# Two of 24 sums of spectra products moved from VectorE to accumulating transfers that GpSimd issues

## The chip, the cores and the metric

The kernel runs on one core of a Trainium2 chip. The metric is device time in microseconds (us) of one execution. Of the kernel before, three runs gave 275.06, 275.24 and 275.45 us; the median is 275.24 us. A further execution was profiled. It took 275.08 us, of which the profile's span, from the first to the last instruction of the program, is 273.3 us; the other 1.8 us lie around it.

A core has five engines that run side by side and tell each other of finished work through semaphores: TensorE (PE: matmuls, with weight loads listed apart as PEld), VectorE (DVE), ScalarE (ACT), GpSimd (POOL) and SyncE (SP, which only issues transfers). Each works through its own instructions in their order. Sixteen DMA engines carry out the transfers.

## The reference

The input `x` is `A_u`, 2048 positions of 640 channels in bf16. Two branches read it and are mixed by a gate for each position:

```python
g = _sigmoid((x * gate_w).sum(-1, keepdims=True))
a = _A_ref(x, A_re, A_im, B_re, B_im, C_re, C_im, log_dt, Dskip)
b = (_gelu(x @ w_gate) * (x @ w_up)) @ w_down        # F = 1728
return g * a + (1 - g) * b
```

`_A_ref` builds for each channel a filter `K` of 2048 lags (128 complex exponentials, summed) and convolves `x` with it along the positions, by the product of their spectra, then adds `u * Dskip`:

```python
K = jnp.einsum("dn,dnl,dn->dl", Cc, P, dB).real      # P = exp(dt * A * l)
Yf = Uf * Kf                                         # spectra of u and K, complex
y = irfft2(Yf)[..., :L].astype(bfloat16) + u * Dskip
```

## The kernel before, in words

**Spectra in blocks.** The kernel cuts the 2048 positions into four blocks of 512 and the filter in the same way. Matmuls with constant cosine and sine matrices make the spectra `Uf[i]` of the blocks and `Kf[j]` of the filter's parts (steps `U...` and `K...`, lines 729 and 742; ScalarE takes them out of PSUM). Output block `c` is the sum over pairs of blocks `i` and filter parts `j = c - i` of complex products. This is done for the channels in two halves `h` of 320. A spectrum tile is 128 partitions of 2 x 4 x 320 values.

**The products.** The function `spectra(c)` does this on VectorE. Names are made of `h`, `c`, `i` and a part: `m0110` is a product for half 0, block 1, input block 1, part 0. Part 0 goes to a tile `P` (two buffers, by `c % 2`), part 1 to `X`. The first pair of a block writes its product straight into `P` or `X` (line 784, 128x2560). Each further pair writes its product into a tile `t` or `t1` (line 787) and is then added: step `s...`, line 788. There are 24 such sums in all. At the end `y...0` and `y...1` (lines 790 and 791, 128x1280) combine `P` and `X` crosswise, and `P` holds the finished spectrum.

**The inverse.** Matmuls with `P` as the moving data bring the block back to positions (`I...`, line 802, 8 matmuls a step). They must end before `P`'s buffer is written for the block after the next.

**The other branch.** Its matmuls run first (line 391); up-products are kept in HBM (`Ud`), come back through a ring of three buffers on the SP queue (`rl...`, line 717) and are multiplied into `H` on VectorE (`hm...`, line 718, 128x1024). `H` is the weight of the down matmuls (`D...`, line 816), which add into the same PSUM as the mixing of the first branch (`Z...`, lines 823 and 824); ScalarE scales and SP stores.

**Order.** All of it is written out by hand: the string `ORDER` is a list of step names, and the steps are issued in its order. Engines keep the order of their own steps; which one waits for which follows from the tiles that they touch. GpSimd has little to do: some memsets and, early on, eight gathers (line 375).

Of the kernel before, what the change touches and what calls it, by code (L numbers as in the profile page):

```python
# [11 lines left out]
ALU = mybir.AluOpType  # L12
# [54 lines left out]
eK010/A ge5.0 ek1.5/D ct1.2/1 ct1.1/2 gl3 lu01 rl10.0 lw13 ct1.6/3 ek1.4/D gl4 ek1.2/D hm4.0 ge1.0 ek1.1/A lwz0 gl5 ct1.0/0  # L67
ek1.0/A hm5.0 gl6 ct1.3/1 ek1.6/A ek1.3/D ge11.0 K002/2 U011/3 eK002/D K012 eK012/A ge12.0 U010/0 eU010/A rl12.0 U013/1
eU013/A gl7 ks.1 m0000 kd.1 g8.1/2 rl2.0 m0001 hm10.0 leu3 eU011/A dg8 rl1.0 gf/1 U012/3 eU012/A ge3.0 y000 g9.1/2 gf1 ge7.0
m0101 y001 g11.1/3 lkb1 lu02 K022/1 U022/0 dg9 gl8 lim1 U021/2 m0100 lkb0 hm12.0 dg11 rl7.0 hm1.0 m0111 leu0 eU022/A K033/3  # L70
eU021/A U023/0 er0 lim0 hm2.0 K020/2 rl3.0 eK033/A eK022/A eU023/A lu03 eK020/A I001/3 s0101 eI001/A rl6.0 U020/1 m0110
K023/0 hm7.0 s0100 rl0.0 g10.1/2 lu10 hm3.0 rl8.0 eU020/A U032/1 ge9.0 y011 eK023/A eU032/A m0221 y010 U030/3 rg0.1 leu1 er1
eU030/A hm6.0 I000/0 U031/1 hm0.0 K021/3 dg10 rl9.0 m0210 U103/2 hm8.0 rl11.0 m0211 eI000/A rg13.1 eU031/A rl13.0 rg7.1 m0220
rg6.1 eU103/A D000/0 K030/1 eK021/A K031/2 hm9.0 eK030/A D000a rg5.1 eK031/A hm11.0 U100/1 ge13.0 eU100/A D001/2 lwe0 er2
K032/3 eK032/A rl11.1 pm0/A hm13.0 pm1/A D001a U101/1 eU101/A I010/3 D000b ge13.1 D001b U033/1 D000c s0220 eI010/A D001c
# [5 lines left out]
eU111/A K101/3 eU122/A hm1.1 lwz1 U120/2 K120/0 eK123/A lwe1 eU120/A rl0.1 rl3.1 s0311 s0310 hm2.1 eK101/A lu13 hm0.1 eK120/A  # L81
hm3.1 U123/1 D021/2 m0320 eU123/A m0321 K111 D020/1 eK111/A U133/3 s0320 K130/0 D021a D020a eK130/A pm3/A pm2/A eU133/A lwd1
s0321 m0330 m0331 s0330 s0331 st010 m1000 U131/0 Z021 D031/3 y030 o021/A eU131/A st021 U121/0 Z020 o020/A y031 D031a I031/1
m1100 eU121/A st020 D030/2 I030/0 eI030/A D030a m1001 m1101 y100 y101 eI031/A Z031 Z030 o030/A o031/A I101/1 m1110 m1111
s1100 s1101 I100/0 eI101/A U132/3 m1210 y111 y110 m1221 m1211 m1220 s1221 s1220 eU132/A D100/1 eI100/A m1201 K132/2 D101/3
U130/0 D101a D100a eU130/A Z101 m1200 Z100 eK132/A s1201 st030 o101/A o100/A st100 s1200 I111/2 m1321 y121 D111/3 I110/0
D111a D110/1 eI111/A D130/2 y120 m1310 m1311 m1320 s1321 Z111 D110a o111/A eI110/A K133/3 eK133/A Z110 st031 o110/A s1320
I121/0 I120/3 m1331 eI121/A m1330 D120/1 D130a s1331 s1330 K131/0 eK131/A m1301 m1300 s1301 eI120/A s1300 st110 st101 st111
# [56 lines left out]
def kernel(  # L145
# [25 lines left out]
    V, A, P, S, G = nc.vector, nc.scalar, nc.tensor, nc.sync, nc.gpsimd  # L171
# [87 lines left out]
    def step(name, fn, job=None, opening=False):  # L259
        assert name not in steps, name  # L260
        steps[name] = fn
        if opening:
            opens[name] = job
# [7 lines left out]
    for i in range(6):  # L271
        step(f"lp{i}", lambda i=i: (A if i == 0 else S).dma_start(out=at["prm"][:, i],
                                                                 in_=PRM[i].rearrange("(p j) n -> p (j n)", p=128)))
# [53 lines left out]
    tt, ts, stt = V.tensor_tensor, V.tensor_scalar, V.scalar_tensor_tensor  # L327
# [333 lines left out]
    for th in range(2):  # L661
        step(f"er{2 + th}", lambda th=th: tt(out=H[th][64:78, 13].rearrange("q (x p) -> q x p", x=2)[:, :, 508:512],
                                             in0=edge_r[64:78, 2 * th:2 * th + 2], in1=edge[:, 2 * th:2 * th + 2], op=ALU.mult))
# [30 lines left out]
    for h in range(2):  # L694
# [3 lines left out]
                                       op=ALU.mult))  # L698
# [49 lines left out]
    for h in range(2):  # L748
# [22 lines left out]
        def spectra(c, h=h, Uf=Uf, Kf=Kf):  # L771
            Pt, X, tb = at["P"][:, c % 2], at["X"], (at["t"], at["t1"])
            fl = (lambda v: v.rearrange("p r m d -> p r (m d)"))
            seq = PAIRS[h][c]
            flip0 = (c - seq[0]) % 2
            for i in seq:
                j = c - i
                for part in range(2):
                    dst, t = (Pt, X)[part], tb[part]
                    row = part ^ (j % 2)  # L780
                    ux = fl(Uf[i])[:, row:row + 1].to_broadcast([128, 2, 4 * W2])
                    kx = fl(Kf[j])
                    if i == seq[0]:
                        step(f"m{h}{c}{i}{part}", lambda dst=dst, ux=ux, kx=kx: tt(out=fl(dst), in0=ux, in1=kx, op=ALU.mult))
                    else:
                        op = ALU.subtract if part and j % 2 != flip0 else ALU.add
                        step(f"m{h}{c}{i}{part}", lambda t=t, ux=ux, kx=kx: tt(out=fl(t), in0=ux, in1=kx, op=ALU.mult))
                        step(f"s{h}{c}{i}{part}", lambda t=t, dst=dst, op=op: tt(out=fl(dst), in0=fl(dst), in1=fl(t), op=op))  # L788
            ops = (ALU.add, ALU.subtract) if flip0 else (ALU.subtract, ALU.add)
            step(f"y{h}{c}0", lambda: tt(out=fl(Pt)[:, 0], in0=fl(Pt)[:, 0], in1=fl(X)[:, 1], op=ops[0]))  # L790
            step(f"y{h}{c}1", lambda: tt(out=fl(Pt)[:, 1], in0=fl(Pt)[:, 1], in1=fl(X)[:, 0], op=ops[1]))
# [69 lines left out]
        for c in range(4):  # L861
            spectra(c)
            inverse(c)
# [38 lines left out]
```

## Time and profile before

| what | value |
|---|---|
| median of three runs | 275.24 us (275.06 to 275.45) |
| profiled execution | 275.08 us, span 273.3 us |
| TensorE busy in the span | 261.3 us |
| VectorE busy | 255.6 us |
| ScalarE busy | 219.4 us |
| GpSimd busy | 36.7 us |
| moved by DMA | 49.05 MB, mean 179 GB/s |
| one sum of a product (line 788), 24 of them | 1.48 us each |

The page of a profile gives shares over the whole span; the kernel has stages with different limits, so a stage is read from the table of busy time by stretch, and the order within it from the timeline. A row of the timeline has the start and the duration in us, the engine, the line, the operation, what it writes and reads, how many instructions are merged in it, and in brackets the engine's idle time ahead of it with what ended it. An instruction's duration holds its tail in the pipeline; the next one starts a little before it ends, so what an instruction costs its engine is the distance to the next start.

### The profile page before, as it was taken

How to read it: one execution, taken by the hardware profiler on the slowest of the kernel's cores; microseconds unless marked ns; L12 is line 12 of the kernel's file. 1: busy time of each engine (PE TensorE's matmuls, PEld its weight loads, DVE VectorE, ACT ScalarE, POOL GpSimd, SP SyncE). 2: the span in 40 equal slices, each digit the busy share in tenths (PEclk: the TensorE clock that was granted, in tenths of full speed). 3: DMA queues.
4: the chain of work that ended last, by engine and by line, in shares of the span. 5: the costliest groups of instructions: out<-in, count | busy, mean ns of one | idle time of the engine just before them, and what ended most of it. 6: DMA issues, size and time to landing. Idle time of an engine off the chain costs nothing.

```text
span 273.3 us, 4927 instructions
## 1 busy us (share of the span) xinstructions
PE 261.3 (96%) x1874; PEld 159.8 (58%) x1889; DVE 255.6 (94%) x330; ACT 219.4 (80%) x300; POOL 36.7 (13%) x23
## 2 busy tenths in 40 slices
PE   4899999999999999999998999999999999999995
PEld 3743444444674444555594557777777777777773
DVE  0899999999989999999999999999999999999971
ACT  3899999999999999999999999999985444305223
POOL 2300301999531000000010000000000000000000
PEclk9999999999999999999999999999999999999999
DMA  7968859864785888887995896978980100101011
GB/s 196 261 184 227 250 140 242 276 208 105 195 272 139 233 265 245 246 287 210 276 288 121 280 252 195 289 202 267 262 246 23 50 0 26 46 2 50 24 50 48
DMA packets 64141, 49.05 MB, mean 179 GB/s; under 512 B 23499, under 2 KB 52982, under 8 KB 64118
## 3 DMA queue, kind: packets, MB, share of 16 engines
q1 hardware_dynamic: 63158, 47.00, 61.0%
q0 software_dynamic: 384, 1.31, 1.8%
q10 hardware_dynamic: 576, 0.43, 0.5%
q8 instruction: 15, 0.25, 0.4%
q14 instruction: 8, 0.07, 0.1%
HBM read 30.44 MB, written 15.67 MB: 169 GB/s over the span
## 4 chain that ended last, share of the span: by engine, by line
PE 71%; ACT 18%; DVE 5%; issue 3%; DMA 2%; SPq 0%; DVEq 0%; ACTq 0%
PE ps L391 24%; PE ps L816 22%; PE ps L802 6%; PE ps L729 6%; PE ps L742 4%; ACT work L396 3%; DVE work L398 2%; ACT work L480 2%; PE ps L537 2%; PE ps L538 2%; ACT work L472 2%; ACT H L709 2%; PE ps L823 2%; ACT work L484 2%; PE ps L824 1%
## 5 line engine op out<-in xcount | busy, mean ns | idle before, releaser
L391 PE MATMUL ps<-xT,Wr 128*128 128x512 bf16 x525 | 118.9, 379 | 3.7 <-DVE work L347 0.7
L391 PEld LDWEIGHTS <-Wr 128*128 128x128 bf16 x540 | 52.6, 98 | 65.7 <-issue 5.0
L396 ACT CAST work<-ps 128x640 bf16<-128x640 f32 (+1 forms) x59 | 47.5, 838 | 11.5 <-PE ps L802 7.4
L375 POOL DMA_INDIRECT early<-in_A_u_dram,back x8 | 31.4, 3929 | 40.7 <-DVE early L382 32.3
L816 PE MATMUL ps<-xT,H 128*128 128x320 bf16 x224 | 32.9, 299 | 0.0
L402 ACT ACTIVATE Wr<-ps,gs 128x320 bf16<-128x320 f32 x30 | 14.0, 527 | 23.0 <-PE ps L824 14.7
L816 PE MATMUL ps<-xT,work 128*128 128x320 bf16 x224 | 32.4, 299 | 0.0
L816 PEld LDWEIGHTS <-H 128*128 128x128 bf16 x224 | 21.9, 98 | 8.5
L816 PEld LDWEIGHTS <-work 128*128 128x128 bf16 x224 | 21.9, 98 | 8.5
L504 ACT ACTIVATE tail<-work 128x1920 bf16<-128x1920 int16 x14 | 25.3, 1821 | 0.4
L525 DVE TENSOR_TENSOR work<-tail,work 128x1920 bf16<-128x1920 bf16 (+1 forms) x22 | 23.4, 1087 | 0.0
L507 ACT ACTIVATE tail<-work 128x1920 bf16<-128x1920 int16 (+1 forms) x12 | 19.5, 1631 | 1.5 <-DVE work L487 1.0
L802 PE MATMUL ps<-work,tail 128*128 128x320 bf16 x128 | 19.5, 299 | 0.0
L492 DVE SCALAR_TENSOR_TENSOR work<-early,tail 128x320 int32<-128x320 f32 x42 | 18.0, 481 | 0.0
L788 DVE TENSOR_TENSOR work<-work,early 128x2560 bf16<-128x2560 bf16 x12 | 17.8, 1481 | 0.0
L788 DVE TENSOR_TENSOR work<-work 128x2560 bf16<-128x2560 bf16 x12 | 17.8, 1480 | 0.0
L729 PEld LDWEIGHTS <-early 128*128 128x128 bf16 x128 | 12.5, 98 | 7.6 <-issue 2.3
L516 DVE TENSOR_TENSOR work<-tail,work 128x1920 bf16<-128x1920 bf16 x14 | 16.1, 1150 | 0.2
L487 DVE TENSOR_SCALAR work<-work 128x960 int32<-128x960 int16 (+1 forms) x26 | 16.1, 624 | 0.1
L398 DVE CAST work<-ps 128x1024 bf16<-128x1024 f32 x13 | 15.7, 1212 | 0.0
L742 PE MATMUL ps<-KTt,early 128*128 128x320 bf16 x80 | 15.5, 299 | 0.0
L802 PEld LDWEIGHTS <-tail 128*128 128x128 bf16 x128 | 12.5, 98 | 4.9
(128 smaller groups left out, 423.1 us busy)
## 6 DMA issues: line engine op xcount, KB each, us to landing
Ud<-work SPq DMA_DIRECT2D x26, 256.0 KB, 2.4
work<-Ud SPq DMA_DIRECT2D x26, 256.0 KB, 3.3
Wr<-in_B_w_gate_dram SPq DMA_DIRECT2D x10, 320.0 KB, 3.7
Wr<-in_B_w_up_dram SPq DMA_DIRECT2D x10, 320.0 KB, 3.9
PMd<-early SPq DMA_DIRECT2D x4, 640.0 KB, 4.9
Gd<-work SPq DMA_DIRECT2D x9, 256.0 KB, 4.7
work<-Gd SPq DMA_DIRECT2D x9, 256.0 KB, 5.0
out_dram<-Wr SPq DMA_DIRECT2D x14, 160.0 KB, 1.9
```

The lines of the kernel that those rows point to most:

```text
L375: G.indirect_dma_start(out=at["ur"][:, e, :], out_offset=None, in_=u2[:, :], in_offset=bass.IndirectOffsetOnAxis(ap=back[:, 2 * c + e:2 * ...
L391: P.matmul(t[:, x, :], lhsT=Wr[:, slot, kt, cols:cols + 128], rhs=xT[:, th, kt, 512 * x:512 * x + 512], start=(kt == 0), stop=(kt == 4))
L396: A.copy(out=out, in_=in_)
L398: V.tensor_copy(out=out, in_=in_)
L504: act(out=T, in_=low16(t)[:, :, :, ::2], func=ACT.Sin, scale=SIN_SCALE)
L507: act(out=T[:, :, 0:n], in_=low16(t[:, :, 0:n])[:, :, :, ::2], func=ACT.Sin, scale=SIN_SCALE)
L525: tt(out=B2[:, :, :, cols].rearrange("p r g x -> p g r x"), in0=Tv if hf == 0 else Tv[:, :, ::-1], in1=e, op=ALU.mult)
L729: P.matmul(t[:, r, 0:W2], lhsT=FM[:, m, e, r], rhs=pm[:, r, e], start=(e == 0), stop=(e == 1))
L742: P.matmul(t[:, r, 0:W2], lhsT=mat[:, r], rhs=KTt[:, q, d], start=(x == 0 and j != 1), stop=(x == len(seq) - 1), skip_group_check=(j == 1))
L788: step(f"s{h}{c}{i}{part}", lambda t=t, dst=dst, op=op: tt(out=fl(dst), in0=fl(dst), in1=fl(t), op=op))
L802: P.matmul(t[:, r, 0:W2], lhsT=IM[:, e, m, r], rhs=Y[:, r, m], start=(m == 0), stop=(m == 3))
L816: P.matmul(t[:, x, 0:W2], lhsT=H[c // 2][:, ft, tk:tk + 128], rhs=at[f"Wd{h}"][:, ft], start=(ft == 0), stop=False)
```

## The change

Two things are changed. For block `c = 1`, in both halves, the sum of part 0 (`s0100` and `s1100`) is no longer an addition on VectorE. GpSimd issues a transfer from `t` to `P` in which the DMA engines add the source to what stands at the destination. And the list of steps is put in another order around both: the products `m0110` and `m1110`, which write `P` first, come earlier, and the transfer stands right behind them.

```diff
-m0101 y001 ... m0100 lkb0 hm12.0 dg11 rl7.0 hm1.0 m0111 leu0 eU022/A K033/3
-eU021/A U023/0 er0 lim0 hm2.0 ... I001/3 s0101 eI001/A rl6.0 U020/1 m0110
-K023/0 hm7.0 s0100 rl0.0 g10.1/2 lu10 hm3.0 rl8.0 ... y011
+m0101 y001 ... m0100 lkb0 hm12.0 dg11 rl7.0 hm1.0 m0111 m0110 s0100 leu0
+eU022/A K033/3 eU021/A U023/0 er0 lim0 hm2.0 ... I001/3 s0101 eI001/A rl6.0
+U020/1 K023/0 hm7.0 rl0.0 g10.1/2 lu10 hm3.0 rl8.0 ... y011
...
-m1100 eU121/A ... m1001 m1101 y100 y101 ... m1110 m1111
-s1100 s1101 I100/0 eI101/A U132/3 m1210 y111 y110
+m1100 eU121/A ... m1001 m1101 m1110 s1100 y100 y101 ...
+m1111 s1101 I100/0 eI101/A U132/3 m1210 y111 y110
...
-                        step(f"s{h}{c}{i}{part}", lambda t=t, dst=dst, op=op: tt(out=fl(dst), in0=fl(dst), in1=fl(t), op=op))
+                        if part == 0 and c == 1:
+                            step(f"s{h}{c}{i}{part}", lambda t=t, dst=dst: G.dma_start(out=fl(dst), in_=fl(t), accum_op=ALU.add,
+                                                                                       max_dma_last_dim=2560))
+                        else:
+                            step(f"s{h}{c}{i}{part}", lambda t=t, dst=dst, op=op: tt(out=fl(dst), in0=fl(dst), in1=fl(t), op=op))
```

Four lines are added, so lines from 788 on carry a number that is higher by 4 in the changed kernel: 788 becomes 792 (and 789 the transfer), 790 and 791 become 794 and 795, 802 becomes 806, 816 becomes 820.

On VectorE around the first sum the order was, with the semaphores that each row waits for (L784: `m0111`, `m0110`; L788: `s0101`, `s0100`; L791: `y011`; L718: H products):

```order
L784 TENSOR_TENSOR work<-work,early 128x2560 [waits DVE_49,Activation_49]
L718 TENSOR_TENSOR H_78<-H_78,work 128x1024 [waits DMAHW1_49,Activation_49]
L788 TENSOR_TENSOR work<-work,early 128x2560 [waits DVE_49]
L784 TENSOR_TENSOR work<-work,early 128x2560
L718 TENSOR_TENSOR H_78<-H_78,work 128x1024 [waits DMAHW0_49,Activation_49]
L788 TENSOR_TENSOR work<-work 128x2560 [waits DVE_49]
L718 TENSOR_TENSOR H_78<-H_78,work 128x1024 [waits DMAHW4_49]
L791 TENSOR_TENSOR work<-work 128x1280 [waits DVE_49]
```

and with the change:

```order
L784 TENSOR_TENSOR work<-work,early 128x2560 [waits DVE_49,Activation_49]
L784 TENSOR_TENSOR work<-work,early 128x2560
L718 TENSOR_TENSOR H_78<-H_78,work 128x1024 [waits DMAHW1_49,Activation_49]
L792 TENSOR_TENSOR work<-work,early 128x2560 [waits DVE_49]
L718 TENSOR_TENSOR H_78<-H_78,work 128x1024 [waits DMAHW0_49,Activation_49]
L718 TENSOR_TENSOR H_78<-H_78,work 128x1024 [waits DMAHW4_49]
L795 TENSOR_TENSOR work<-work 128x1280 [waits DMASW0_49,DVE_49]
```

One L788 is gone, the second L784 stands directly behind the first, and the combine L795 now waits for a semaphore of the GpSimd queue's transfers (`DMASW0`).

Around the second sum VectorE had this order (L784: `m1110`, `m1111`, `m1210`; L790 and L791 are first `y100`, `y101`, and at the end `y111`, `y110`):

```order
L787 TENSOR_TENSOR early<-tail,work 128x2560
L790 TENSOR_TENSOR work<-work 128x1280 [waits DVE_49]
L791 TENSOR_TENSOR work<-work 128x1280
L784 TENSOR_TENSOR work<-early,tail 128x2560 [waits PE_49]
L784 TENSOR_TENSOR work<-early,tail 128x2560 [waits DVE_49]
L788 TENSOR_TENSOR work<-work 128x2560 [waits DVE_49]
L788 TENSOR_TENSOR work<-work,early 128x2560 [waits DVE_49]
L784 TENSOR_TENSOR work<-early,work 128x2560 [waits PE_49]
L791 TENSOR_TENSOR work<-work 128x1280 [waits DVE_49]
```

and has this one with the change:

```order
L787 TENSOR_TENSOR early<-tail,work 128x2560
L784 TENSOR_TENSOR work<-early,tail 128x2560 [waits PE_49]
L794 TENSOR_TENSOR work<-work 128x1280 [waits DVE_49]
L795 TENSOR_TENSOR work<-work 128x1280
L784 TENSOR_TENSOR work<-early,tail 128x2560 [waits DVE_49]
L792 TENSOR_TENSOR work<-work,early 128x2560 [waits DVE_49]
L784 TENSOR_TENSOR work<-early,work 128x2560 [waits PE_49]
L795 TENSOR_TENSOR work<-work 128x1280 [waits DMASW1_49,DVE_49]
```

The product that waits for TensorE moved ahead of the two combines of the block before, one L788 is gone, and the later L795 waits for the transfer.

On GpSimd's queue the last instructions are now, where only the three memsets stood (L695 and L630 zero rows of `Wd` and of `H`):

```order
L695 MEMSET xT 64x320 [waits PE_49]
L789 DMA work<-work 128x2x1280 [waits DVE_49,Activation_49]
L630 MEMSET work 64x1024 [waits PE_49]
L695 MEMSET xT 64x320 [waits PE_49]
L789 DMA work<-work 128x2x1280 [waits DVE_49]
```

The memset of L630 now stands behind the first transfer. The order of TensorE, ScalarE and SP is what it was.

More of the change, by code (lines that the diff above doesn't have):

```diff
@@ L69 @@
 eU013/A gl7 ks.1 m0000 kd.1 g8.1/2 rl2.0 m0001 hm10.0 leu3 eU011/A dg8 rl1.0 gf/1 U012/3 eU012/A ge3.0 y000 g9.1/2 gf1 ge7.0
-m0101 y001 g11.1/3 lkb1 lu02 K022/1 U022/0 dg9 gl8 lim1 U021/2 m0100 lkb0 hm12.0 dg11 rl7.0 hm1.0 m0111 leu0 eU022/A K033/3
-eU021/A U023/0 er0 lim0 hm2.0 K020/2 rl3.0 eK033/A eK022/A eU023/A lu03 eK020/A I001/3 s0101 eI001/A rl6.0 U020/1 m0110
-K023/0 hm7.0 s0100 rl0.0 g10.1/2 lu10 hm3.0 rl8.0 eU020/A U032/1 ge9.0 y011 eK023/A eU032/A m0221 y010 U030/3 rg0.1 leu1 er1
+m0101 y001 g11.1/3 lkb1 lu02 K022/1 U022/0 dg9 gl8 lim1 U021/2 m0100 lkb0 hm12.0 dg11 rl7.0 hm1.0 m0111 m0110 s0100 leu0
+eU022/A K033/3 eU021/A U023/0 er0 lim0 hm2.0 K020/2 rl3.0 eK033/A eK022/A eU023/A lu03 eK020/A I001/3 s0101 eI001/A rl6.0
+U020/1 K023/0 hm7.0 rl0.0 g10.1/2 lu10 hm3.0 rl8.0 eU020/A U032/1 ge9.0 y011 eK023/A eU032/A m0221 y010 U030/3 rg0.1 leu1 er1
 eU030/A hm6.0 I000/0 U031/1 hm0.0 K021/3 dg10 rl9.0 m0210 U103/2 hm8.0 rl11.0 m0211 eI000/A rg13.1 eU031/A rl13.0 rg7.1 m0220
@@ L83 @@
 s0321 m0330 m0331 s0330 s0331 st010 m1000 U131/0 Z021 D031/3 y030 o021/A eU131/A st021 U121/0 Z020 o020/A y031 D031a I031/1
-m1100 eU121/A st020 D030/2 I030/0 eI030/A D030a m1001 m1101 y100 y101 eI031/A Z031 Z030 o030/A o031/A I101/1 m1110 m1111
-s1100 s1101 I100/0 eI101/A U132/3 m1210 y111 y110 m1221 m1211 m1220 s1221 s1220 eU132/A D100/1 eI100/A m1201 K132/2 D101/3
+m1100 eU121/A st020 D030/2 I030/0 eI030/A D030a m1001 m1101 m1110 s1100 y100 y101 eI031/A Z031 Z030 o030/A o031/A I101/1
+m1111 s1101 I100/0 eI101/A U132/3 m1210 y111 y110 m1221 m1211 m1220 s1221 s1220 eU132/A D100/1 eI100/A m1201 K132/2 D101/3
 U130/0 D101a D100a eU130/A Z101 m1200 Z100 eK132/A s1201 st030 o101/A o100/A st100 s1200 I111/2 m1321 y121 D111/3 I110/0
```

## The prediction, made before the changed kernel was run

> **What bounds the kernel now.** I read the page's shares first, then the busy time by stretch, then what TensorE (PE) waited for.
>
> ```profile
> PE 261.3 (96%) x1874; PEld 159.8 (58%) x1889; DVE 255.6 (94%) x330; ACT 219.4 (80%) x300; POOL 36.7 (13%) x23
> ...
> core 0: us, PE busy (x) PEld busy (x) DVE busy (x) ACT busy (x) POOL busy (x), PEclk, DMA share, GB/s
> 166.00:200.00 34.00, 34.00 (x253) 24.50 (x251) 33.81 (x39) 32.91 (x52) 0.00 (x0) 1.00 0.80 237
> 200.00:240.00 40.00, 40.00 (x296) 28.81 (x295) 40.00 (x34) 19.70 (x39) 0.00 (x0) 1.00 0.21 61
> 240.00:265.00 25.00, 25.00 (x186) 18.00 (x184) 24.76 (x20) 6.94 (x13) 0.00 (x0) 1.00 0.09 27
> ...
> PE ps L296 <- ACT Wr L402: 1.2, 1, 1.2
> PE ps L823 <- ACT work L396: 0.2, 1, 0.2
> ```
>
> The first row has two engines near full, PE at 96% and VectorE (DVE) at 94%; a share does not say which of them sets the end. The rows by stretch do for the part that the change touches: from 166 to 265 us PE is busy in every microsecond (34.00 of 34.00, 40.00 of 40.00, 25.00 of 25.00) at a granted clock of 1.00. The last two rows, from the list of PE's waits, are the only waits there of the final stretch, both after 265 us and both for ScalarE. So from 166 us on PE is a queue without a hole. DVE is as busy, but works ahead of it. Two things follow. DVE time that is saved there shortens nothing, and DVE lateness that uses up its lead costs PE time that no later gap gives back.
>
> **What the change removes, and what that is worth.** Here is DVE around the first sum, and the weight load at which PE next needs DVE's output.
>
> ```profile
> 155.02 1.48 DVE L784 TENSOR_TENSOR work<-work,early 128x2560 bf16<-128x2560 bf16 x1
> 156.42 0.68 DVE L718 TENSOR_TENSOR H<-H,work 128x1024 bf16<-128x1024 bf16 x1
> 157.02 1.48 DVE L788 TENSOR_TENSOR work<-work,early 128x2560 bf16<-128x2560 bf16 x1
> 158.42 1.48 DVE L784 TENSOR_TENSOR work<-work,early 128x2560 bf16<-128x2560 bf16 x1
> 159.82 0.68 DVE L718 TENSOR_TENSOR H<-H,work 128x1024 bf16<-128x1024 bf16 x1
> 160.43 1.48 DVE L788 TENSOR_TENSOR work<-work 128x2560 bf16<-128x2560 bf16 x1
> 161.83 0.68 DVE L718 TENSOR_TENSOR H<-H,work 128x1024 bf16<-128x1024 bf16 x1
> 162.43 0.82 DVE L791 TENSOR_TENSOR work<-work 128x1280 bf16<-128x1280 bf16 x1
> 163.17 1.48 DVE L787 TENSOR_TENSOR early<-work,early 128x2560 bf16<-128x2560 bf16 x1
> 164.57 0.81 DVE L790 TENSOR_TENSOR work<-work 128x1280 bf16<-128x1280 bf16 x1
> 165.31 1.28 DVE L718 TENSOR_TENSOR H<-H,work 128x1024 bf16<-128x1024 bf16 x2
> ...
> 166.80 0.91 PEld L816 LDWEIGHTS <-H 128*128 128x128 bf16 x7
> ```
>
> A sum is the L788 row at 160.43: it takes 1.48 us, and the next instruction starts 1.40 us after it. Two sums are 2.8 us of DVE. They are worth 0 on the end, because PE's full rows cover them. (If DVE set the end they would be worth 2.8 us; that is a rival below.)
>
> **What it adds at the first place.** The product s0100 adds (L784 at 158.42) moves up to 156.42, directly behind the one at 155.02, and ends at 156.42 + 1.48 = 157.90. The transfer is issued then. DVE meanwhile does an H product, the other sum, and two more H products: 0.60 + 1.40 + 0.61 + 0.60 = 3.21 us by the spacing of the rows. The combine y011 (now L795, before at 162.43) is thus ready to run at 157.82 + 3.21 = 161.03, and it waits for the landing. Everything of DVE stands behind that wait: y011, a product, y010, and the two H products of 165.31, which end at 166.59. PE loads the second of these as a weight at 166.80, so DVE's lead is 0.21 us. DVE is 1.40 us ahead of its old times when it reaches y011. **The threshold:** a landing up to 161.03 + 1.40 + 0.21 = 162.64 costs nothing, and each microsecond after it costs PE one microsecond.
>
> One H product (156.42) comes 1.4 us later, to 157.82, and so does the load that takes its buffer: the SP queue's L717 goes from 157.50 to 158.9.
>
> ```profile
> 157.50 3.35 SPq L717 DMA_DIRECT2D work<-Ud  x2
> ...
> DMA to landing us min/median/max: 2.7/3.2/3.7
> ```
>
> With the longest of these, 3.7 us, that load lands at 162.6; its reader comes at 161.03 + 0.74 + 1.40 + 0.74 = 163.9 at the earliest. Cost 0, hidden by 1.3 us. The second load under that row follows the H product of 159.82, which does not move.
>
> **How long does the transfer take?** The trace has no accumulating transfer and none within SBUF. The nearest rows:
>
> ```profile
> Ud<-work SPq DMA_DIRECT2D x26, 256.0 KB, 2.4
> PMd<-early SPq DMA_DIRECT2D x4, 640.0 KB, 4.9
> early<-in_A_u_dram,back POOLq DMA_INDIRECT x8, 4.0
> ...
> q0 software_dynamic: 384, 1.31, 1.8%
> ...
> DMA to landing us min/median/max: 2.9/4.0/26.1
> ...
> GB/s 196 261 184 227 250 140 242 276 208 105 195 272 139 233 265 245 246 287 210 276 288 121 280 252 195 289 202 267 262 246 23 50 0 26 46 2 50 24 50 48
> ...
> 161.00:164.00 3.00, 2.95 (x18) 1.59 (x17) 3.00 (x4) 3.00 (x5) 0.36 (x1) 1.00 0.97 293
> 222.00:228.00 6.00, 6.00 (x46) 4.33 (x45) 6.00 (x6) 3.65 (x7) 0.00 (x0) 1.00 0.09 27
> ```
>
> GpSimd's eight gathers moved 1.31 MB, 160 KB each, and took 4.0 us from issue to landing (median; 2.9 the least). This transfer has 128 partitions of 2560 bf16, 640 KB, so 480 KB more. Between the first two rows 384 KB cost 2.5 us, 6.5 ns per KB; DMA engines are 0.97 busy while this transfer is under way, so a price from a loaded run fits. Estimate: 4.0 + 480 x 0.0065 = **7.1 us**. Low end: 2.9 us and the 480 KB at the highest slice of the GB/s row, 288: 2.9 + 1.7 = 4.6 us. High end: the destination must be read as well as written, so twice the extra bytes: 4.0 + 2 x 3.1 = 10.2 us. Below nothing is excluded, since PE has no idle time to recover. I take the middle one: 640 KB is nearest to the PMd row, the fixed part to the gathers.
>
> **Two rules of the Trainium skill** bear on this price, and the sum does not use them. The page "DMA: Bandwidth & Descriptors", section "Anatomy of one DMA — SWDGE (gpsimd) path", fits such a transfer as 2.0 us plus bytes over 436 GB/s: an estimate of 3.5 us here, by which nothing would change. For 160 KB it gives 2.4 us where the gathers above took 4.0, so the trace does not agree with it. The page "SBUF — State Buffer", section "Who interferes with whom", also of the Trainium skill, has a DVE operation in a two-port mode lock GpSimd out of the shared ports, while one with two inputs in SBUF only contends with GpSimd's reads; the rows under the third rival agree with both, and by it the third rival would not come about here.
>
> GpSimd starts its instruction 0.27 us after DVE's release (45.72 + 0.81 to 46.80, rows below), so the clock runs from 158.17. Landing: 158.17 + 7.1 = 165.27, which is **2.6 us** past the threshold (ends: 162.77, 0.1 us; 168.37, 5.7 us). On GpSimd's own queue a memset of L630 now stands behind this issue, at about 159 instead of 140 us; its reader is DVE's L662 at 194.68. Cost 0.
>
> ```profile
> 194.68 0.15 DVE L662 TENSOR_TENSOR work<-edge_r,picks 14x8 bf16<-14x8 bf16 x1
> ```
>
> **The second place.** DVE and PE there, and where their next meetings are:
>
> ```profile
> 220.92 2.88 DVE L784 TENSOR_TENSOR work<-early,tail 128x2560 bf16<-128x2560 bf16 x2
> 227.93 0.81 DVE L791 TENSOR_TENSOR work<-work 128x1280 bf16<-128x1280 bf16 x1
> 263.98 0.82 DVE L791 TENSOR_TENSOR work<-work 128x1280 bf16<-128x1280 bf16 x1
> ...
> 219.37 1.25 PE L802 MATMUL ps<-work,tail 128*128 128x320 bf16 x8
> 223.44 2.34 PE L802 MATMUL ps<-work,tail 128*128 128x320 bf16 x16
> 265.55 2.34 PE L802 MATMUL ps<-work,tail 128*128 128x320 bf16 x16
> ```
>
> The product m1110 now goes ahead of y100 and y101. It writes a buffer that PE reads until 219.37 + 1.25 = 220.62, so it waits there and starts at 220.66; this wait gives back the 1.4 us of the sum. y100 then ends at 222.9 and y101 at 223.6. PE reads them from 223.44 and, for the second half of the first eight matmuls, from 223.98: in time by 0.5 and 0.4 us. y111 can start at 220.66 + 1.40 + 2 x 0.73 + 3 x 1.40 = 227.7, against 227.93 before. The transfer starts at 222.07 + 0.08 + 0.27 = 222.4, with DMA engines 0.09 busy; 4.6 to 7.1 us bring 227.0 to 229.5, so y111 is 0 to 1.6 us late. The tightest later meeting is the last: DVE's 263.98 + 0.82 = 264.80 for the fifth matmul after 265.55, at 266.09, a lead of 1.3 us. Cost 0 to 0.3; I take 0. With 10.2 us it is 4.7 - 1.3 = 3.4.
>
> **The sum.** Profiled execution 275.08 us (span 273.3, 1.8 around it) + 2.6 + 0 = 277.7; the median of the runs is 0.16 above that execution: **277.8 us**, the forecast, for 5.2 to 10.2 us a transfer 275.9 to 281.
>
> **Rivals.**
> 1. *The first transfer is hidden.* It lands within 5.0 us of its issue (threshold 4.5, and 0.55 us, 0.2%, is about what can be told from no change). For: the least gather, and the low end of 4.6. Against: DMA engines 0.97 busy just then. Time 275.2.
> 2. *DVE sets the pace, and the change is faster.* For: DVE is 40.00 of 40.00 busy. If its lead at the last L802 were 0, the two sums would come off the end: 275.2 - 2.8 = 272.4. Against: that lead is 1.3 us, and PE shows no gap to close.
> 3. *GpSimd cannot make the descriptors while DVE runs.* The place is GpSimd's issue itself:
>
> ```profile
> 45.72 0.81 DVE L382 TENSOR_TENSOR early<-early 128x1280 bf16<-128x1280 bf16 x1
> 70.12 2.42 DVE L516 TENSOR_TENSOR work<-tail,work 128x1920 bf16<-128x1920 bf16 x2
> ...
> 46.80 24.04 POOL L375 DMA_INDIRECT early<-in_A_u_dram,back  x1 [16.77 <-DVE early L382]
> 71.15 0.95 POOL L375 DMA_INDIRECT early<-in_A_u_dram,back  x1 [0.30 <-issue]
> ```
>
> One gather took 24.04 us beside an unbroken row of mixed DVE work; the next took 0.95 beside two TENSOR_TENSORs of L516. DVE does only TENSOR_TENSOR around both new transfers, which speaks against. If it holds, issue begins when DVE itself stops: 161.03 + 7.1 = 168.1, 5.5 late, and 227.7 + 7.1 = 234.8, 6.9 - 1.3 = 5.6 late: 286.3. With 4.6 us each it is 3.0 + 3.1: 281.3. Middle 283.8.
>
> **Chances.** Forecast 0.57, hidden 0.27, faster 0.06, starved 0.10. So slower by over 0.2%: 0.67; within: 0.27; faster: 0.06. The forecast's own range is 275.9 to 281. The whole one goes down to 275.0 for the hidden case and up to 282.0 for some of the starved one; outside are the faster case and most of the starved.
>
> **What would show it.** Right: y011 (L795) with an idle gap before it of some 4 us, ended by the accumulating transfer; a PE gap of about 2.6 us before the L820 group near 167; no gap over 2 us at the second L795; PE busy as long as before. Hidden: no gap at L795. Starved: POOL's L789 rows far over 1 us. The prediction is wrong if the landing is 4.5 us or less, if the sums' time shows at the end, or if the two waits together cost over 6 us.

## The result, and the profile after

The changed kernel takes **281.44 us** (median of 4 runs, 280.90 to 281.83) against 275.16 us; the ratio is 1.0225, 95% interval 1.0206 to 1.0244. It is slower by 6.3 us where 2.6 us were forecast. The profiled execution took 280.9 us, its span 279.0 us, 5.7 us more than before.

VectorE (DVE) around the first transfer, GpSimd's issues, and the landings, with the changed kernel's line numbers:

```profile
154.99 2.88 DVE L784 TENSOR_TENSOR work<-work,early 128x2560 bf16<-128x2560 bf16 x2
161.34 0.69 DVE L718 TENSOR_TENSOR H<-H,work 128x1024 bf16<-128x1024 bf16 x1 [0.86 <-DMA work<-Ud]
166.78 0.82 DVE L795 TENSOR_TENSOR work<-work 128x1280 bf16<-128x1280 bf16 x1 [4.75 <-DMA work<-work]
169.66 1.29 DVE L718 TENSOR_TENSOR H<-H,work 128x1024 bf16<-128x1024 bf16 x2
...
158.49 1.33 POOL L789 DMA_DIRECT2D work<-work  x1 [40.44 <-DVE H L718]
159.28 1.52 POOL L630 MEMSET work<- 64x1024 bf16 x1
228.21 1.23 POOL L789 DMA_DIRECT2D work<-work  x1 [65.62 <-DVE work L784]
...
DMA to landing us min/median/max: 5.7/7.0/8.2
```

The waiting combine (L795) starts at 166.78 instead of 162.43, after 4.75 us of idle time; the first transfer landed 8.2 us after its issue, the second 5.7. There is a wait in front of that already: an H product idles 0.86 us for its load (`work<-Ud`), which the kernel before never did there. VectorE reaches this product about 1.4 us sooner than before; its load is only a little later.

TensorE (PE), its waits and its clock, with three rows of the kernel before at the end:

```profile
PE ps L729 <- DMA tail<-PMd: 3.2, 1, 3.2
PE ps L820 <- DVE H L718: 0.5, 1, 0.5
...
169.74 0.72 PE L729 MATMUL ps<-tail,early 128*128 128x320 bf16 x4 [3.24 <-DMA tail<-PMd]
171.01 1.86 PE L820 MATMUL ps<-xT,H 128*128 128x320 bf16 x7 [0.55 <-DVE H L718]
173.72 1.58 PE L820 MATMUL ps<-xT,H 128*128 128x320 bf16 x7
175.68 1.11 PE L820 MATMUL ps<-xT,H 128*128 128x320 bf16 x7
...
166.00:175.00 9.00, 5.22 (x25) 2.83 (x24) 8.22 (x9) 4.22 (x8) 0.00 (x0) 0.81 0.57 180
...
166.39 0.71 PE L729 MATMUL ps<-tail,early 128*128 128x320 bf16 x4
166.94 1.11 PE L816 MATMUL ps<-xT,H 128*128 128x320 bf16 x7
169.92 1.11 PE L816 MATMUL ps<-xT,H 128*128 128x320 bf16 x7
```

Two things stand here that the prediction did not have. The longer of PE's waits is not for VectorE but for `tail<-PMd`, a load of spectra input on the SP queue that has nothing to do with the sums. And after the idle time seven matmuls take 1.86 us, later 1.11: the row of busy time from 166 to 175 us has a granted clock of 0.81.

The load `tail<-PMd` is issued at 160.9 us in both kernels. The trace has 16 completions for it: before, they came from 163.84 to 164.48 us, 1.9 us ahead of the matmul that reads it; in the changed kernel 15 of them came from 166.71 to 167.64 and the last at 169.69, 8.8 us after the issue. Why that one came 2 us behind the others is open.

PE's lateness can be read off step by step against the last three rows. The spectrum step L729 ran at 166.39 before and runs at 169.74: 3.35 us. The first H group ran at 166.94 and runs at 171.01: 4.07. The third H group ran at 169.92 and runs at 175.68: 5.76. After that it stays (span 5.7). So about 4.1 us are waits and about **1.7 us matmuls at a lower clock**. The other three timed runs have a mean clock of 0.988 instead of this one's 0.994, more time at the low clock, and take longer, up to 281.83 us.

The second transfer cost next to nothing:

```profile
226.41 1.49 DVE L784 TENSOR_TENSOR work<-early,tail 128x2560 bf16<-128x2560 bf16 x1 [1.81 <-PE ps L806]
234.02 0.83 DVE L795 TENSOR_TENSOR work<-work 128x1280 bf16<-128x1280 bf16 x1 [0.19 <-DMA work<-work]
```

The moved product waits 1.81 us for PE, which gives the saved sum back, and the combine waits 0.19 us. PE shows no gap there.

### The profile page after: what moved, and what is told of

Read it like the earlier page. It is cut to its first block, busy times and chain, and to the rows that moved or that the text cites. A ratio compares the mean times of both kernels' runs of the same rounds, so it can differ in the third digit from the quotient of the medians.

```text
span 279.0 us, 4945 instructions
## 1 busy us (share of the span) xinstructions
PE 263.8 (95%) x1889; PEld 159.9 (57%) x1889; DVE 253.4 (91%) x328; ACT 219.8 (79%) x300; POOL 39.4 (14%) x25
## 4 chain that ended last, share of the span: by engine, by line
PE 65%; DVE 21%; DMA 7%; issue 4%; ACT 3%; SPq 0%; DVEq 0%; ACTq 0%
PE ps L391 22%; PE ps L820 22%; PE ps L806 5%; PE ps L742 4%; PE ps L729 4%; DMA Ud<-work 3%; DVE work L398 3%; DMA work<-work 3%; DVE work L784 2%; DVE work L500 2%; DVE H L718 2%; PE ps L312 2%; PE ps L827 2%; PE ps L828 1%; DVE work L512 1%
## 5 line engine op out<-in xcount | busy, mean ns | idle before, releaser
L820 PE MATMUL ps<-xT,H 128*128 128x320 bf16 x224 | 34.1, 306 | 0.5 <-DVE H L718 0.5
L729 PEld LDWEIGHTS <-early 128*128 128x128 bf16 x128 | 12.4, 98 | 11.1 <-DMA tail<-PMd 3.6
L789 POOL DMA_DIRECT2D work<-work x2 | 2.6, 1280 | 106.1 <-DVE work L784 65.6
```

What stands on the lines that cost most here:

```text
L729: P.matmul(t[:, r, 0:W2], lhsT=FM[:, m, e, r], rhs=pm[:, r, e], start=(e == 0), stop=(e == 1))
L820: P.matmul(t[:, x, 0:W2], lhsT=H[c // 2][:, ft, tk:tk + 128], rhs=at[f"Wd{h}"][:, ft], start=(ft == 0), stop=False)
```

## The experiments

The first theory after the result (A): the late first landing holds VectorE back, PE idles, and the idle time lowers its clock. Rivals: the second transfer has a share (B); the order alone costs (C). Later ones are about the two waits near 167 us.

**The first transfer alone.**

```diff
-if part == 0 and c == 1:
+if part == 0 and c == 1 and h == 0:
```

with the old order in half 1.

> The changed kernel with the first transfer (s0100) alone; half 1 is as before. Theory A: all of the 6.2 us comes from the first place: a late landing holds VectorE at the combine, TensorE waits for a load and for an H product (3.5 + 0.7 us), and 1.5 us more go to matmuls at half the granted clock right after that idle time. It expects 281.4 us, within 0.6. Rival B: the second transfer has a share, by slowing what runs beside it: it expects 279 to 280.5 us.

281.84 us, ratio 1.0229 (1.0203 to 1.0254). All of the loss comes from the first place. In its profile the two waits are divided otherwise, with nearly the same sum (3.81 us against 3.79); here the last completion of `tail<-PMd` came 0.2 us behind the one before it, not 2:

```profile
168.54 0.72 PE L729 MATMUL ps<-tail,early 128*128 128x320 bf16 x4 [1.81 <-DMA tail<-PMd]
171.25 2.05 PE L820 MATMUL ps<-xT,H 128*128 128x320 bf16 x7 [2.00 <-DVE H L718]
```

**The second transfer alone** (`h == 1`, old order in half 0).

> The changed kernel with the second transfer (s1100) alone; half 0 is as before. Theory A expects no difference to the kernel before (275.2, within 0.6): the transfer lands near 228, VectorE waits at most 1 us at the combine, and TensorE's queue has no hole. Rival B expects 276 to 278 us. A rival by which VectorE's saved 1.4 us reach the end expects 273.8.

275.35 us, ratio 1.0002 (0.9992 to 1.0012). No difference. A sum taken off VectorE there neither costs nor brings anything.

**The order alone, both sums on VectorE.**

```diff
-if part == 0 and c == 1:
+if False:
-m1101 m1110 s1100 y100 y101
+m1101 m1110 y100 y101 s1100
```

> The new order of the products with both sums on VectorE again (the second sum stands behind the two combines of the block before). Theory A expects no difference to the kernel before (275.2, within 0.6): the order alone costs nothing, the transfers do. Rival C, that the moved products themselves make TensorE wait, expects 276 to 278 us.

276.03 us, ratio 1.0026 (1.0015 to 1.0037): 0.7 us, a little over what was expected, and PE shows where:

```profile
PE ps L729 <- DMA tail<-PMd: 0.7, 1, 0.7
```

The same load is 0.7 us late with no transfer at all. With both sums on VectorE the new order puts an H product 2.9 us later, at 159.31 instead of 156.42; the ring load that waits for it on the SP queue holds up what stands behind, so that `tail<-PMd` is issued 1.5 us later (first row before, second this run):

```profile
160.90 0.53 SPq L754 DMA_DIRECT2D tail<-PMd  x1
...
162.40 0.53 SPq L754 DMA_DIRECT2D tail<-PMd  x1
```

That alone would fit into the 1.9 us by which the load was early. But its last completion also came later, at 167.13, 4.7 us after the issue instead of 3.6; the other 15 were there at 165.85. In the changed kernel the issue stands at 160.88, as before, so this delay of the issue is no part of its 6.3 us.

**Matmuls of constants where PE idles.**

```diff
+P.matmul(PS[bank[j]][:, 0, W2:512], lhsT=ident, rhs=picks[:, 0:192], start=True, stop=True)   # 44 times
-m0210 U103/2
+m0210 fill/2 U103/2
```

> The changed kernel with 44 matmuls of constants (192 columns each, into columns of a bank that nobody reads) put ahead of the spectrum step at which TensorE idles 3.2 us. Theory A expects the granted clock to stay at 1.00 and the waits to stay: 275.2 + 4.2 = 279.4 us, 2 us less than the changed kernel. A rival by which the half clock comes from something other than the idle time (the transfer itself, or power) expects the same 281.4 us or more.

279.54 us, ratio 1.0149 (1.0123 to 1.0175), 1.9 us below the changed kernel; its stretch from 166 to 175 us:

```profile
166.00:175.00 9.00, 9.00 (x85) 7.36 (x84) 8.65 (x9) 5.41 (x10) 0.00 (x0) 1.00 0.59 184
```

The clock stays at 1.00, and VectorE's wait is still there (4.62 us). The first H group runs at 170.57, 3.6 us later than before, and no lateness is added over the next groups, where the changed kernel lost 1.7 us more. That the median is so close to A's 279.4 is in part chance: the last completion of the load came at 168.29 in the profiled execution, the constants kept PE until 169.96, and another 1.0 us was lost later, most of it at 189 us in a wait for ScalarE. That the low clock follows from PE's idle time is shown, since only PE's idle time was changed.

**VectorE's wait off PE's path.** The H products that PE needs are done before the combine that waits:

```diff
-U032/1 ge9.0 y011 eK023/A eU032/A m0221 y010 U030/3 ... hm6.0 ... U031/1 hm0.0 K021/3
+U032/1 ge9.0 eK023/A eU032/A m0221 U030/3 ... hm6.0 ... U031/1 hm0.0 y011 y010 K021/3
```

> The changed kernel with the two H products, which the first down matmuls need, and one product ahead of the combine that waits for the first transfer (y010 follows it). VectorE's wait then holds up no weight of TensorE near 167 us. Theory A, with the load of spectra input as a second late piece: TensorE still waits 2.3 to 3.5 us for that load at the spectrum step, and 1.5 us of half clock follow: 279 to 280.3 us. Rival D, that the load's lateness is of no consequence and VectorE's wait alone set the time: 276.0 us or less.

278.45 us, ratio 1.0097 (1.0059 to 1.0134), just under the range that A gave, and not at D's 276. PE still waits, for the load:

```profile
168.81 0.72 PE L729 MATMUL ps<-tail,early 128*128 128x320 bf16 x4 [2.17 <-DMA tail<-PMd]
...
166.59 0.69 DVE L718 TENSOR_TENSOR H<-H,work 128x1024 bf16<-128x1024 bf16 x1 [2.67 <-DMA work<-Ud]
```

VectorE did not get on either: the H product moved ahead stood 2.67 us waiting for its own load. Of the four runs, two at a mean clock of 1.000 took 277.01 and 277.76 us, two at 0.994 took 279.15 both. The wait of 2.17 us is that of a run at 0.994; the waits of the other runs are not on record. So in one and the same kernel the clock went down in half of the runs.

**The late load off PE's path.** Two spectrum steps change places (`U103` and `U033`), so that PE needs `tail<-PMd` later:

```diff
-m0210 U103/2 ... eU103/A ... U033/1 ... eU033/A
+m0210 U033/2 ... eU033/A ... U103/1 ... eU103/A
```

> The changed kernel with the spectrum step that waits for the late load exchanged with another one whose input is there early; VectorE's order is untouched. Theory A: VectorE's wait still keeps the H product back by 4.2 us, so the load's wait falls away and the other becomes longer by as much, with the half clock behind it: 281.4 us, within 0.7. Rival E, that the load's wait adds to the other: 3.5 us less, 278 us.

281.07 us, ratio 1.0206 (1.0189 to 1.0223); not different from the changed kernel. The other wait became as long as both had been:

```profile
171.25 2.05 PE L820 MATMUL ps<-xT,H 128*128 128x320 bf16 x7 [3.95 <-DVE H L718]
```

**Both edits.**

> Both edits: H products ahead of the waiting combine, and the spectrum step exchanged. Theory A: no wait near 167 us that is longer than 0.5 us, no half clock; VectorE is some 1.6 us late behind the combine, of which 0.9 us pass its lead at a later H product: 276.2 us, between 275.2 and 277. A rival by which the transfer slows TensorE's other inputs in general (all loads on the DMA engines) expects 278 us or more.

278.38 us, ratio 1.0105 (1.0079 to 1.0131). Theory A is wrong here by 2 us; the rival's 278 fits. No wait for the transfer is left on PE's path, and yet:

```profile
168.50 0.69 DVE L718 TENSOR_TENSOR H<-H,work 128x1024 bf16<-128x1024 bf16 x1 [4.35 <-DMA work<-Ud]
...
169.25 1.12 PE L820 MATMUL ps<-xT,H 128*128 128x320 bf16 x7 [2.02 <-DVE H L718]
```

VectorE waited 0.2 us for the transfer and 4.35 us for a ring load (`work<-Ud`). So there are two mechanisms: the combine's own wait, and **the loads of the SP queue beside the transfer**, which land late. In the profiled executions the loads alone made PE wait 2.0 us here and 2.2 us with the H products ahead, and the combine's wait made it wait 3.95 us with the steps exchanged; in the changed kernel the two overlap.

How late `tail<-PMd` is can be read from its time from issue to landing: in the kernel before, in this run, and in the two runs that follow, where the transfer is a plain copy and where it has half the bytes:

```profile
DMA to landing us min/median/max: 3.6/3.6/3.6
...
DMA to landing us min/median/max: 8.1/8.1/8.1
...
DMA to landing us min/median/max: 5.3/5.3/5.3
...
DMA to landing us min/median/max: 5.1/5.1/5.1
```

The lateness shrinks with what the transfer asks of the DMA engines.

**Plain copies instead of adds** (`accum_op=ALU.add` left out, so the sum is not formed and block 1 holds one product less).

> The changed kernel with both transfers as plain copies that GpSimd issues (the add is left out, so P holds the last product alone in block 1). Theory A, that the add makes each packet longer since the destination is read too: packets of 2560 bytes take under 150 ns instead of 221 to 229 ns, the first transfer lands after some 6.5 us instead of 8.2, the second after 4.5 instead of 5.7. Rival F, that queue and issue set the time and the add costs nothing: packets and landings as with the add.

277.24 us in one run. The landings are 6.1 us for the first and 3.5 us for the second, where A gave 6.5 and 4.5; rival F has fallen:

```profile
DMA to landing us min/median/max: 3.5/4.8/6.1
...
169.06 1.12 PE L820 MATMUL ps<-xT,H 128*128 128x320 bf16 x7 [1.86 <-DVE H L718]
...
q0 software_dynamic: 672, 2.62, 3.0%
```

The last row, GpSimd's queue, had 1.8% of the 16 engines' span before; of the changed kernel it is this one:

```profile
q0 software_dynamic: 928, 2.62, 4.2%
```

For the same bytes 1.2% of 275.5 us more here, 3.3 us or 1.65 a transfer; with the add 2.4% of 279.0 us, 6.7 us or 3.3 a transfer. With the add the DMA engines spend twice the time. In the trace's packets of the first transfer it is 208 ns for 5120 bytes against 221 ns for 2560. The packet size changed with it, so A's 150 ns for a plain packet of 2560 bytes was not measured. But small packets are not dear in themselves: in the trace of the kernel before, the SP queue's plain packets have medians of 55 ns at 1280 bytes, 84 at 2048 and 196 at 5120, by which a plain one of 2560 would take some 100 ns (an estimate between the last two). So the doubling is the add's.

**Half of each sum by the transfer**, the other half on VectorE:

```diff
+G.dma_start(out=fl(dst)[:, 1], in_=fl(t)[:, 1], accum_op=ALU.add, max_dma_last_dim=2560)
+tt(out=fl(dst)[:, 0], in0=fl(dst)[:, 0], in1=fl(t)[:, 0], op=ALU.add)
```

> The changed kernel with half of each sum by the transfer (the half that the waiting combine reads, 320 KB) and the other half by VectorE (128x1280). Theory A, a transfer's time is a fixed 2.7 us to its first packet plus its packets beside the loads: 8 packets an engine instead of 16 land some 2.2 us sooner, about 164.3 us; TensorE loses about 1.5 to 2.2 us instead of 4.2, in a wait too short for the half clock: 277 us, between 276 and 278. A rival by which a transfer's time is fixed (issue, queue, completion) expects 279 us or more.

277.26 us, ratio 1.0074 (1.0057 to 1.0091), inside A's range, at an undisturbed clock. The landing came after 5.4 us, and both waits shrank together:

```profile
166.94 0.72 PE L729 MATMUL ps<-tail,early 128*128 128x320 bf16 x4 [0.41 <-DMA tail<-PMd]
168.25 1.12 PE L821 MATMUL ps<-xT,H 128*128 128x320 bf16 x7 [0.59 <-DVE H L718]
```

PE is 1.3 us late behind them (168.25 against 166.94), a little less than A gave. The rest of the 2.1 us comes later in the profiled execution, most of it, 0.55 us, at the second place, where VectorE's half of the sum stands ahead of the two combines that PE needs. So the agreement of the total is in part chance.

**The first transfer 2.6 us earlier**, ahead of two H products and the other product.

```diff
-m0100 lkb0 hm12.0 dg11 rl7.0 hm1.0 m0111 m0110 s0100 leu0
+m0100 lkb0 m0110 s0100 hm12.0 dg11 rl7.0 hm1.0 m0111 leu0
```

> The changed kernel with the first product and its transfer 2.6 us earlier, ahead of two H products and of the other product; the transfer has 2.6 us more before the combine that waits for it. Theory A, each microsecond past the threshold costs one and the half clock comes only behind a long idle time: the landing is at 164.2 us, TensorE loses 1.6 us and keeps its clock: 276.8 us, between 276 and 278. A rival by which the loads beside the transfer set the loss, wherever it stands, expects 278.5 us or more.

278.84 us, ratio 1.0132 (1.0104 to 1.0161): the rival, not A. The transfer no longer holds anything up (VectorE waits 0.2 us at the combine), but other loads now bear the loss:

```profile
166.08 1.26 PE L729 MATMUL ps<-work,early 128*128 128x320 bf16 x8 [2.52 <-DMA work<-PMd]
...
165.05 0.69 DVE L718 TENSOR_TENSOR H<-H,work 128x1024 bf16<-128x1024 bf16 x1 [4.27 <-DMA work<-Ud]
```

Another load of spectra input is late, and a ring load again. Giving the transfer room moves the loss from one wait to another.

That the DMA engines are the place can be seen in their share, before and in the changed kernel (first row before, second after):

```profile
164.00:167.00 3.00, 3.00 (x24) 2.17 (x23) 3.00 (x5) 3.00 (x6) 0.00 (x0) 1.00 0.54 167
...
164.00:167.00 3.00, 2.51 (x19) 1.57 (x16) 0.22 (x1) 3.00 (x6) 0.00 (x0) 1.00 1.07 296
```

Before, the DMA engines were about half idle after 164 us (0.54). With the transfer they are full three microseconds longer (packets overlap, so a share can pass 1). At the second place 0.09 was in use before (222 to 228 us), and nothing else waited.

## Why the prediction was right or wrong

- **What bounds the kernel: right.** No run came out faster than before. The second transfer alone, 1.0002, is the plainest case: VectorE's saved sum had no worth.
- **The price of a transfer: right in kind, low.** The forecast was 7.1 us with ends of 4.6 and 10.2; measured 8.2 under load and 5.7 without. Of the two terms, the fixed part and the bytes, the bytes were too small: half of them landed after 5.4 us, so 320 KB cost 2.8 us, an estimate of 8.7 ns per KB where the sum had 6.5. By the Trainium skill's fit in "DMA: Bandwidth & Descriptors", section "Anatomy of one DMA — SWDGE (gpsimd) path", 3.5 us is the estimate for 640 KB; the plain copy at the second place, where the DMA engines had little else to do, landed after 3.5 us, so the trace agrees for that, while an add took 5.7 there and the loaded stretch 2.5 more.
- **The threshold: right.** With a landing at 158.49 + 8.2 = 166.7 it gives 166.7 - 162.64 = 4.1 us; PE's first H group was late by 4.07. Issue was 0.3 us later than estimated. The sign that the prediction gave for it, a gap of PE ahead of that group, is only 0.55 us long in the profile: most of the idle time stands one step earlier, at the load. With the spectrum steps exchanged the gap is where it was looked for, 3.95 us.
- **"Cost 0" for the loads: wrong.** The prediction followed one ring load through the queue, by its landing time in an unburdened run, and none of the others. That one landed at 162.9, close to the 162.6 forecast. The others are where a step failed in kind: the transfer takes 3.3 us of each DMA engine in a stretch where these were 0.97 busy, and the loads issued from 160.5 us on are pushed back, `tail<-PMd` by 5.2 us. In the changed kernel this is hidden behind VectorE's wait (the swap alone brought nothing), so it did not move the number; it is why none of the reorderings here repairs the change.
- **The sum left a term out; this is the step that failed.** The span grew by 5.7 us where 2.6 were forecast, and the larger part of what is missing stands here. A wait of PE was priced one to one. PE loses more: after it the matmuls run at the low clock, 1.7 us in the profiled execution and more in the runs at 0.988. PE's first H group was late by 4.07 where the forecast had 2.63 (165.27 - 162.64); these 1.44 us come from the landing and the issue. With them the sum is made up: 2.63 + 1.44 + 1.69 = 5.76, the lateness of the third H group.
- **The second place: right**, point by point: the moved product waited for PE (1.81 us), the combine for 0.19 us, PE not at all. One slip of the sum stayed without effect: the 281 us for 10.2 us a transfer leaves out the 3.4 us that the prediction had worked out for this place at that price.
- **The starved rival: fallen.** Both issues took 1.33 and 1.23 us while VectorE ran TENSOR_TENSORs. What held the one gather for 24 us is not settled by these runs.
- Not predicted, and 0.7 us with both sums on VectorE: **the order itself**, by the same load; the changed kernel does not have that delay of its issue.

Still open is how the wait for the load and for the transfer would divide if each had its own engines; no run could keep the loads unburdened and the transfer late.

## What to carry to other kernels

A transfer that takes work off an engine pays with time of the DMA engines, and its price is read from the loads that it stands among: ask of each load in flight by how much it is early, not only whether the new transfer is in time. Work taken off an engine that only runs ahead of the bounding one is worth nothing, whatever its busy share says. And a wait of TensorE of about 2 us or more, as the clock behaved in these runs, is priced with the low clock that may follow it.

## What was not expected of the hardware

- **The clock follows idle time well below a whole quiet window.** In this kernel the low clock came in pieces of 3.4 us: in the changed kernel's records at half clock from 171.2 to 174.7 us, with the first transfer alone from 170.4 for 6.8 us. By the waits of the profiled executions and the mean clocks of all runs, a wait of 0.7 us left the clock at 1.00, one of 1.86 and one of 2.02 us too; in a kernel with one of 2.17 us it went down in two of four runs, and so it did in the one with 2.52 us (the first transfer earlier); with 1.81 + 2.00, 3.24 + 0.55 and 3.95 us it went down in every run. The profiled execution with 2.52 us kept it, the one with 2.17 us did not, so the length of the wait does not decide alone. The clock's changes in these traces lie whole multiples of 3.41 us apart. From where the records begin, near 10 us, to the end of the spans, every fall of the clock follows a window of 3.41 us in which PE was idle for 2.17 us or more, and no other window had more than 1.84 us. Here are the window before the low clock in the changed kernel, then the one with the wait of 2.17 us, then two that share the 2.52 us:

```profile
core 0: us, PE busy (x) PEld busy (x) DVE busy (x) ACT busy (x) POOL busy (x), PEclk, DMA share, GB/s
167.83:171.25 3.42, 0.96 (x6) 0.52 (x7) 3.42 (x5) 0.71 (x2) 0.00 (x0) 1.00 0.11 36
...
166.07:169.49 3.42, 1.25 (x10) 0.70 (x8) 2.90 (x4) 1.41 (x3) 0.00 (x0) 1.00 1.04 363
...
161.99:165.40 3.41, 1.57 (x8) 0.48 (x5) 0.35 (x1) 2.39 (x2) 0.36 (x1) 1.00 1.05 345
165.40:168.82 3.42, 2.74 (x21) 1.98 (x22) 3.42 (x5) 1.98 (x3) 0.00 (x0) 1.00 0.89 301
```

PE was idle for 2.46 and 2.17 us of the first two windows, and the next window had the half clock; it was idle for 1.84 and 0.68 us of the last two, and the clock stayed. So the same wait can cost the clock or not, by where a window's edge cuts it; that this divides the unprofiled runs is likely, not shown. The Trainium skill's page "TensorE: Matmul & The Clock Gate", section "What's actually happening", has a free-running window of about 3.4 us and names an idle window as what lowers the clock. The trace agrees with the window of 3.4 us, but PE was idle for only part of it.
- **An accumulating transfer within SBUF** of 640 KB keeps each DMA engine busy for about 3.3 us, twice a plain copy's 1.65, and lands after 5.7 us at the least here.
